# Two expert rounds in one visit, and GpSimd for every key feature

## The chip, the cores and the metric

The kernel runs on one core of a Trainium2 chip. The metric is the device time of one launch in microseconds (us). Three timed runs of the kernel before took 267.41, 268.63 and 268.75 us; the median is 268.63.

## The reference

2048 tokens of width 1024 go through two branches, mixed by a gate per token:

```
g = sigmoid(sum(x * gate_w))                       # one gate per token
a = linear attention(x) @ wo                       # 32 heads of 32
b = x + (one token's expert output, added to its row)
out = g * a + (1 - g) * b
```

In the attention the features of keys and queries are `phi(k) = [softmax(k w_phi), softmax(-k w_phi)]`, 64 numbers a head; `kv = sum over tokens of phi(k) v`, `z = sum of phi(k)`, and each query's output is `phi(q) kv / (phi(q) z)`.

The expert works on one token only: the one with the largest router score `x @ w_r`. Its row `xs` gives `y = (silu(xs @ w_gate) * (xs @ w_up)) @ w_down`, with 3584 hidden columns, times the sigmoid of its score. The three weights are 7.3 MB each, so this branch is mostly a matter of streaming weights.

## The kernel before, in words

**Stages.** First the values of all 16 token tiles (128 tokens each) are computed on TensorE (`k_v`), together with the router and gate scores; in the same stretch `w_phi` is folded into the key and query weights (`fold`, `qfold`), so that later one product gives the features' exponents. `route` and `route_row` find the row index of the expert's token. Then come 32 key steps, `i` = 0 to 31, and 32 query steps with the output product.

**A key step.** One unit `u` is half the heads of one token tile. `feats(u)` issues eight matmuls of 512 columns (L615) into one of two PSUM buffers; ScalarE writes two exponentials (L620, L621) into `e` (four buffers); VectorE sums them (`ssum`, L625) and takes the reciprocal (L629); one engine multiplies (`phi`, L633; six buffers). Which engine does that is chosen at L632: VectorE for unit 3, GpSimd for all others. Five steps later (`LAG`) `k_kv(u)` adds the unit's `phi` times `v` into PSUM with eight small matmuls (L646), for which `phi` is the loaded weight.

**The row index.** `route_row` is called in step 0, after `feats(0)`. VectorE reduces 16 candidates to one number (L367 to L374) and copies it to an integer tile `ixi` (L376). SP loads a register from that tile (L377) and issues the DMA of the token's row (L378). At the very end of the program GpSimd loads the same index into a register for a rarely taken path (L893). `one_hot` and its followers (L386 to L421) turn the index into masks in steps 16 to 23.

**The expert's first two products.** They are done in four rounds, `ffn_gu(r, bufs)`. A round loads weights into buffers, named by letters: W and V are the halves of one buffer, X and Y of another that is free after the value stage, D is one of two buffers that held weights to be folded, A one of a ring of three, of which two hold folded query weights until these are transposed (L331, `qfold_turn`, at steps 4 and 7). Rounds 0 to 2 have four buffers of 1 MB and 32 matmuls of 32 weight columns (L511), round 3 has two buffers and 16 matmuls. Round 1 has a `gate` and an `up` piece in each buffer. Then ScalarE copies the result out (L516), and SP stores it into `gT` (L520), in four DMAs for round 0 and one for each of the others. `GU` says at which steps rounds are visited: 9, 16 and 23, with rounds 2 and 3 together at 23. Round 0's weights are asked for at step 0.

**Order.** The program's order gives priorities. A planner sets the order of each engine's instructions from estimated durations, and puts an instruction that is ready earlier in the program first; on the chip each engine, and SP's queue of DMA issues, runs its list in that order. `tc.issue_after(ins)` adds edges for the planner: what is issued in the block on the engine of `ins` comes behind `ins`.

Of the kernel before, what the change touches and what calls it, by code (L numbers as in the profile page):

```python
# [11 lines left out]
U32 = mybir.dt.uint32  # L12
ALU = mybir.AluOpType
ACTF = mybir.ActivationFunctionType
AX = mybir.AxisListType
PSUM = bass.MemoryType.PSUM
ET = mybir.EngineType

P = 128
S = 2048  # L20
D = 1024
H = 32
DH = 32
# [4 lines left out]
HH = 16  # L28
# [132 lines left out]
def q_heads(wqf, kb, hf):  # L161
    return wqf[:, kb, hf * 512:(hf + 1) * 512].rearrange("p (r c f) -> p c r f", r=4, f=DH)


def _bc(ap, shape):
    return ap.unsqueeze(len(shape) - 1).to_broadcast(shape)
# [3 lines left out]
def kernel(  # L170
# [4 lines left out]
    nc = tc.nc  # L175
# [7 lines left out]
    const = ctx.enter_context(tc.tile_pool(name="const", bufs=1))  # L183
# [78 lines left out]
    moe = {}  # L262
# [101 lines left out]
    def route_row():  # L364
        mrow = moe["mrow"]
        mxv = const.tile([1, 1], F32, name="mxv")
        nc.vector.tensor_copy(out=mxv[:], in_=moe["rs"][0:1, 0:1])  # L367
        nc.vector.tensor_reduce(out=mxv[:], in_=mrow[:, :, 0], axis=AX.X, op=ALU.max)
        cnd = const.tile([1, NT], F32, name="cnd")
        nc.vector.tensor_scalar(out=cnd[:], in0=mrow[:, :, 0], scalar1=mxv[:, 0:1], scalar2=float(2 * S),  # L370
                                op0=ALU.is_lt, op1=ALU.mult)
        nc.vector.tensor_tensor(out=cnd[:], in0=cnd[:], in1=mrow[:, :, 1], op=ALU.add)
        ixf = const.tile([1, 1], F32, name="ixf")
        nc.vector.tensor_reduce(out=ixf[:], in_=cnd[:], axis=AX.X, op=ALU.min)  # L374
        ixi = const.tile([1, 1], U32, name="ixi")
        nc.vector.tensor_copy(out=ixi[:], in_=ixf[:])  # L376
        idx_sp = nc.values_load(ixi[0:1, 0:1], engines=[ET.SP], min_val=0, max_val=S - 1)  # L377
        nc.sync.dma_start(out=rows[0:KB, :], in_=x2[bass.ds(idx_sp, 1), :].rearrange("o (a b) -> (o a) b", b=P))  # L378
        moe["ix"] = (ixi, ixf)
# [43 lines left out]
    def one_hot_row():  # L423
        ixi, ixf = moe["ix"]
        ixm = const.tile([1, 1], F32, name="ixm")
        nc.vector.tensor_copy(out=ixm[:], in_=moe["rs"][0:1, 0:1])
        nc.vector.tensor_single_scalar(out=ixm[:], in_=ixf[:], scalar=float(TOH * P), op=ALU.is_lt)
        nc.vector.tensor_tensor(out=ixm[:], in0=ixm[:], in1=ixf[:], op=ALU.mult)
        ixu = const.tile([1, 1], U32, name="ixu")
        nc.vector.tensor_copy(out=ixu[:], in_=ixm[:])  # L430
        moe["ixu"] = ixu

    def range_flag():
        rm = const.tile([P, 1], F32, name="rm")
        nc.vector.tensor_reduce(out=rm[:], in_=rmn[:], axis=AX.X, op=ALU.min)
        nc.vector.tensor_copy(out=nbb[:, 0:1], in_=rm[:])
# [40 lines left out]
    def ffn_mid():  # L477
        sg = const.tile([P, NFB], F32, name="sg")
        nc.scalar.activation(out=sg[:], in_=ffn_ps[:, 0:28], func=ACTF.Exp, scale=-1.0)
        nc.vector.tensor_scalar_add(out=sg[:], in0=sg[:], scalar1=1.0)  # L480
        nc.vector.reciprocal(out=sg[:], in_=sg[:])
        nc.vector.tensor_tensor(out=sg[:], in0=sg[:], in1=ffn_ps[:, 0:28], op=ALU.mult)
        nc.vector.tensor_tensor(out=hh[:], in0=sg[:], in1=ffn_ps[:, 28:56], op=ALU.mult)

    def gu_load(r, kp, where):
        def part(w, a0, src, k0, nk, col, n):
            nc.sync.dma_start(out=w[:, a0:a0 + nk * n * 512].rearrange("p (k f) -> p k f", k=nk) if n == 4 or nk == 4 else
                              w.rearrange("p (k f) -> p k f", k=2)[:, :, a0:a0 + n * 512],
                              in_=src[:, k0:k0 + nk, col * 512:(col + n) * 512])
        w = wbuf(where)  # L490
        gate_load(w[0:1, 0:1])
        k0 = 2 * kp
        if r == 0:
            part(w, 0, wg_v, k0, 2, 0, 4)
        elif r == 1:
            part(w, 0, wg_v, k0, 2, 4, 3)
            part(w, 1536, wu_v, k0, 2, 0, 1)
        elif r == 2:
            part(w, 0, wu_v, k0, 2, 1, 4)
        else:  # L500
            part(w, 0, wu_v, 4 * kp, 4, 5, 2)
        return w

    def ffn_gu(r, bufs):
        ws = moe.pop("gu0", None) or [gu_load(r, k, b) for k, b in enumerate(bufs)]
        acc = psB.tile([P, 512], F32, name="facc", tag="pB")
        for k, w in enumerate(ws):
            for q in range(2):
                for g in range(4):
                    kb = 4 * k + 2 * q + g // 2 if r == 3 else 2 * k + q  # L510
                    nc.tensor.matmul(acc[32 * g:32 * g + 32, :], lhsT=xs32[:, kb, :],  # L511
                                     rhs=w[:, (q * 4 + g) * 512:(q * 4 + g + 1) * 512], start=(k == 0 and q == 0),
                                     stop=(k == len(ws) - 1 and q == 1),
                                     tile_position=(0, 32 * g), skip_group_check=True)
        gs = wk.tile([P, 512], F32, name="gs", tag="junk", bufs=2)
        nc.scalar.copy(out=gs[:], in_=acc[:])  # L516
        g0 = 16 * r
        step = 4 if r >= 1 else 1
        for g in range(0, 4, step):
            nc.sync.dma_start(out=gT[g0 + 4 * g:g0 + 4 * (g + step), :], in_=gs[32 * g:32 * (g + step):32, :])  # L520
# [89 lines left out]
    def feats(u, wf, is_q):  # L610
        t, hf = divmod(u, 2)
        pk = psA.tile([P, HH, DH], F32, name="pq" if is_q else "pk", tag="pA")
        pkf = pk[:].rearrange("p h f -> p (h f)")
        for kb in range(KB):
            nc.tensor.matmul(pk[:].rearrange("p (c r) f -> p c r f", r=4) if is_q else pkf,  # L615
                             lhsT=xT[:, kb, t * P:(t + 1) * P],
                             rhs=q_heads(wf, kb, hf) if is_q else wf[:, kb, hf * 512:(hf + 1) * 512],
                             start=(kb == 0), stop=(kb == KB - 1))
        e = wk.tile([P, HH, 2, DH], BF, name="e", tag="e", bufs=4)
        nc.scalar.activation(out=e[:, :, 0, :], in_=pk[:], func=ACTF.Exp)  # L620
        nc.scalar.activation(out=e[:, :, 1, :], in_=pk[:], func=ACTF.Exp, scale=-1.0)  # L621
        moe["e"] = e
        e2 = e[:].rearrange("p h s f -> p (h s) f")
        ssum = sm.tile([P, HH * 2], F32, name="ssum", tag="ssum")
        nc.vector.tensor_reduce(out=ssum[:], in_=e2, axis=AX.X, op=ALU.add)  # L625
        if u % 8 == 0:
            moe["rq"] = sm.tile([P, 8, HH * 2], F32, name="rq", tag="rq", bufs=2)
        rs = moe["rq"][:, u % 8, :]
        nc.vector.reciprocal(out=rs, in_=ssum[:])  # L629
        moe["rs"] = rs  # L630
        phi = wk.tile([P, HH, 2, DH], BF, name="phi", tag="phi", bufs=6)
        eng = nc.vector if not is_q and u == 3 else nc.gpsimd  # L632
        eng.tensor_tensor(out=phi[:].rearrange("p h s f -> p (h s) f"), in0=e2,  # L633
                          in1=_bc(rs, [P, HH * 2, DH]), op=ALU.mult)
        if u % 8 == 7:
            g = u // 8 + 4 * is_q
            nc.vector.tensor_reduce(out=rmn[:, g:g + 1], in_=moe["rq"][:].rearrange("p n h -> p (n h)"),
                                    axis=AX.X, op=ALU.min)
        return phi
# [133 lines left out]
                qfold(*PACKS[t, n])  # L773
    LAG = 5
    QT0, QT1 = (4, 7)
    GU = (9, 16, 23)
    TU = 29
    DN, DN2 = NU + 6,3
    TF, TNUM, TWO, TKV = 1.73, 0.27, 1.73, 0.27
# [5 lines left out]
    i = 0  # L785
    while i < 2 * NU or n_next < NU or wos:
        if i in GU:
            r = GU.index(i)
            ffn_gu(r, ('WVAD', 'DXYA', 'WVAD')[r])
            if r == 2:  # L790
                ffn_gu(3, "AA")
        if i == DN - 3:
            nc.scalar.copy(out=hh32[0:1, 0, 0:1], in_=moe["e"][0:1, 0, 1, 0:1])
            nc.scalar.copy(out=hh32[:], in_=hh[:].unsqueeze(2).to_broadcast([P, NFB, 32]))
# [15 lines left out]
        if i < NU:  # L810
            kst[i] = feats(i, wkf, False)
# [7 lines left out]
        if NU <= i < 2 * NU:  # L819
            q_turn(i - NU, feats(i - NU, wqf, True))  # L820
            pe += TF
            fend[i - NU] = pe
# [5 lines left out]
        if i in (QT0, QT1):  # L828
            h = 4 * (i == QT1)
# [3 lines left out]
        if i == TU:  # L833
            ffn_turn()
            ffn_mid()
        if i == 0:
            route_row()
        if i == 7:
            xs_turn()
# [6 lines left out]
        if i == NU + 18:  # L846
            one_hot_row()
# [25 lines left out]
        if pe >= wo_at:  # L873
# [13 lines left out]
            if (t, nh) == (TOH - 1, 1):  # L887
                q_store(0)
                add_row(moe["y2c"][:, 0, :], nc.values_load(moe["ixu"][0:1, 0:1], engines=[ET.Pool], min_val=0,
                                                            max_val=TOH * P - 1))  # L890
        i += 1
    main.close()
    ip = nc.values_load(moe["ix"][0][0:1, 0:1], engines=[ET.Pool], min_val=0, max_val=S - 1)  # L893
    with tc.If(moe["fv"] > 0):
        general_path(tc, A_wqkv, A_w_phi, A_wo, x2, out2, gate, omg, moe["y2c"][:, 1, :], ip, xT, wqf, ident, BDm)
    keep.close()
# [30 lines left out]
```

## Time and profile before

| | |
|---|---|
| timed runs | 267.41, 268.63, 268.75 us |
| profiled execution | 267.2 us, its span 265.5 us |
| TensorE busy | 258.7 us, 97% of the span |
| VectorE busy | 181.4 us, 68% |
| ScalarE busy | 125.9 us, 47% |
| GpSimd busy | 126.3 us, 48% |
| chain that ended last | TensorE 94%, ScalarE 2%, DMA 1%, VectorE 1%, issue 1% |
| DMA | 58.45 MB, mean 220 GB/s |

The span runs from the first to the last instruction of one execution; the execution's own time is 1.7 us longer. Engines are PE (TensorE), PEld (its weight loads), DVE (VectorE), ACT (ScalarE), POOL (GpSimd) and SP (the queue that issues most DMAs). "Chain that ended last" follows the work back from the last instruction, at each step to what released it. The clock granted to TensorE was full in all of the span.

### The profile page before, as it was taken

The page shows a single profiled execution, that of the slowest core. Times are in us where ns is not written, and L with a number is a line of the kernel's source. Part 1 is how long each engine was busy: PE and PEld are TensorE (multiplying, and loading weights), DVE is VectorE, ACT ScalarE, POOL GpSimd, SP SyncE. Part 2 cuts the span into 40 slices and gives each one's busy share as a digit, 9 for nine tenths or more (in the row PEclk, how much of TensorE's full clock was granted, in tenths as well). Part 3 has the DMA queues.
Part 4 walks back from the last instruction along what each step waited for, and adds up shares of the span by engine and source line. Part 5 has one row for each costly group of instructions (what it writes and reads, how often), then busy time and mean ns, then how long its engine had stood idle before and what let it go on. Part 6 is the DMA issues. An engine that isn't in the chain of part 4 may idle for free.

```text
span 265.5 us, 5323 instructions
## 1 busy us (share of the span) xinstructions
PE 258.7 (97%) x1992; PEld 139.3 (52%) x2015; DVE 181.4 (68%) x314; ACT 125.9 (47%) x259; POOL 126.3 (48%) x86
## 2 busy tenths in 40 slices
PE   8999999999999999999999999999999999999994
PEld 3666766765444454545555455455444544544442
DVE  3000323325789785998788789799898797898872
ACT  3153333337864555554556776447362553435210
POOL 6000000000074999579989887655535555455001
PEclk9999999999999999999999999999999999999999
DMA  6989999939999869999969998997999797889642
GB/s 235 247 133 191 165 190 187 173 78 329 395 348 199 204 101 399 398 336 333 358 232 338 147 247 180 219 202 137 254 216 202 150 236 145 202 150 201 158 120 67
DMA packets 110970, 58.45 MB, mean 220 GB/s; under 512 B 93580, under 2 KB 98780, under 8 KB 110940
## 3 DMA queue, kind: packets, MB, share of 16 engines
q1 hardware_dynamic: 108140, 53.39, 82.9%
q10 hardware_dynamic: 2768, 4.67, 6.6%
q8 instruction: 17, 0.28, 0.4%
q14 instruction: 13, 0.11, 0.1%
q0 software_dynamic: 32, 0.00, 0.0%
HBM read 31.27 MB, written 4.20 MB: 134 GB/s over the span
## 4 chain that ended last, share of the span: by engine, by line
PE 94%; ACT 2%; DMA 1%; DVE 1%; issue 1%; DVEq 0%
PE pq L615 21%; PE po L719 21%; PE pk L615 19%; PE pv L575 18%; PE kvps L646 3%; PE num L680 3%; PE facc L511 2%; PE pW L311 1%; PE pv L597 1%; PE small_ps L529 1%; DMA shv<-in_A_x_dram 1%; PE kvps L597 1%; ACT kvps L335 1%; DVE wfT L328 0%; PE kvps L323 0%
## 5 line engine op out<-in xcount | busy, mean ns | idle before, releaser
L633 POOL TENSOR_TENSOR phi<-e,rq 128x1024 bf16<-128x1024 bf16 x63 | 119.6, 1913 | 66.0 <-DVE rq L629 48.4
L625 DVE TENSOR_REDUCE ssum<-e 128x32 f32<-128x1024 bf16 x64 | 77.4, 1210 | 14.6 <-ACT e L621 14.5
L615 PEld LDWEIGHTS <-xT 128*128 128x128 bf16 x512 | 47.3, 97 | 52.6 <-issue 1.4
L615 PE MATMUL pq<-wqf,xT 128*128 128x512 bf16 x256 | 60.3, 379 | 0.0
L615 PE MATMUL pk<-wkf,xT 128*128 128x512 bf16 x245 | 59.4, 379 | 0.6
L719 PE MATMUL po<-wo_sb,oT 128*128 128x512 bf16 (+2 forms) x252 | 58.4, 372 | 0.6
L575 PE MATMUL pv<-wv_sb,xT 128*128 128x256 bf16 (+2 forms) x336 | 51.1, 307 | 0.0
L575 PEld LDWEIGHTS <-xT 128*128 128x128 bf16 x336 | 31.7, 97 | 15.3 <-issue 0.5
L582 ACT CAST v_all<-pv 128x384 bf16<-128x384 f32 (+1 forms) x45 | 20.1, 448 | 35.2 <-PE pv L575 29.4
L719 PEld LDWEIGHTS <-oT 128*128 128x128 bf16 x264 | 23.9, 98 | 23.3
L620 ACT ACTIVATE e<-pq 128x512 bf16<-128x512 f32 x32 | 18.9, 592 | 36.2 <-PE pq L615 35.7
L313 DVE CAST wkf<-pW 128x512 bf16<-128x512 f32 x16 | 10.3, 686 | 32.9 <-PE pW L311 32.9
L620 ACT ACTIVATE e<-pk 128x512 bf16<-128x512 f32 x32 | 19.1, 597 | 28.5 <-PE pk L615 21.9
L723 DVE SCALAR_TENSOR_TENSOR oo<-po,gate,xg 128x512 bf16<-128x512 f32 (+2 forms) x33 | 24.0, 728 | 4.4 <-PE po L719 4.3
L453 POOL COPY wch<-shv 1x1 bf16<-1x1 bf16 x3 | 0.4, 178 | 53.8 <-DMA shv<-in_A_wqkv_dram 53.8
L629 DVE RECIPROCAL rq<-ssum 128x32 f32<-128x32 f32 x64 | 21.8, 342 | 1.3
L685 DVE TENSOR_TENSOR o_sb<-num,rden 128x512 bf16<-128x512 f32 x32 | 21.6, 674 | 0.8
L621 ACT ACTIVATE e<-pk 128x512 bf16<-128x512 f32 x32 | 18.9, 592 | 0.0
L621 ACT ACTIVATE e<-pq 128x512 bf16<-128x512 f32 x32 | 18.9, 590 | 0.0
L704 ACT ACTIVATE xg<-xin,omg 128x1024 f32<-128x1024 bf16 x16 | 18.4, 1149 | 0.4
L680 PEld LDWEIGHTS <-phT 128*128 128x128 bf16 x256 | 12.4, 98 | 7.8 <-issue 0.5
L646 PEld LDWEIGHTS <-phi 128*128 128x128 bf16 x256 | 11.8, 98 | 7.6 <-issue 0.8
(132 smaller groups left out, 151.9 us busy)
## 6 DMA issues: line engine op xcount, KB each, us to landing
wch<-in_B_w_down_dram SPq DMA_DIRECT2D x7, 1024.0 KB
wch<-in_B_w_up_dram SPq DMA_DIRECT2D x6, 1024.0 KB
wch<-in_B_w_gate_dram SPq DMA_DIRECT2D x4, 1024.0 KB
xin<-in_A_x_dram ACTq DMA_DIRECT2D x16, 256.0 KB
out_dram<-oo SPq DMA_DIRECT2D x30, 128.0 KB
wch<-in_B_w_gate_dram SPq DMA_DIRECT2D x4, 768.0 KB
wv_sb<-in_A_wqkv_dram SPq DMA_DIRECT2D x8, 256.0 KB
wo_sb<-in_A_wo_dram SPq DMA_DIRECT2D x1, 2048.0 KB
```

The source lines that it names most:

```text
L575: nc.tensor.matmul(pv[:, 0:hi - lo], lhsT=xT[:, kb, t * P:(t + 1) * P], rhs=wv_sb[:, kb, lo:hi], start=(kb == 0), stop=(kb == KB - 1))
L582: nc.scalar.copy(out=v_all[:, t, h0:h1, 0:DH], in_=pv[:, 0:(h1 - h0) * DH].rearrange("p (h d) -> p h d", d=DH))
L615: nc.tensor.matmul(pk[:].rearrange("p (c r) f -> p c r f", r=4) if is_q else pkf, lhsT=xT[:, kb, t * P:(t + 1) * P], rhs=q_heads(wf, kb, h ...
L620: nc.scalar.activation(out=e[:, :, 0, :], in_=pk[:], func=ACTF.Exp)
L621: nc.scalar.activation(out=e[:, :, 1, :], in_=pk[:], func=ACTF.Exp, scale=-1.0)
L625: nc.vector.tensor_reduce(out=ssum[:], in_=e2, axis=AX.X, op=ALU.add)
L629: nc.vector.reciprocal(out=rs, in_=ssum[:])
L633: eng.tensor_tensor(out=phi[:].rearrange("p h s f -> p (h s) f"), in0=e2, in1=_bc(rs, [P, HH * 2, DH]), op=ALU.mult)
L680: nc.tensor.matmul(num[:, pl * 66:pl * 66 + 66], lhsT=phT[:, pl, :], rhs=KV[hf][:, pl, :], start=True, stop=True)
L685: nc.vector.tensor_tensor(out=st["o"][:, hf * HH:(hf + 1) * HH, :].rearrange("p (r h) d -> p r h d", h=2), in0=nv[:, :, :, 0:DH], in1=rden ...
L719: nc.tensor.matmul(po[:, 0:w], lhsT=st["oT"][:, kb, :], rhs=moe["wo"][:, kb, sl], start=(kb == 0), stop=(kb == KB - 1))
L723: nc.vector.scalar_tensor_tensor(out=o_out[:, 0:w], in0=po[:, 0:w], scalar=gate[:, t:t + 1], in1=st["xg"][:, sl], op0=ALU.mult, op1=ALU.add)
```

## The change

Rounds 0 and 1 of the expert are visited together at step 14 (rounds 2 and 3 stay at 23). GpSimd multiplies unit 3 too. `route_row` is called in step 1 instead of step 0. Each key unit's sum is issued behind the reciprocal of the unit before, and unit 2's behind the copy of the index to `ixi`. A second integer copy of the index, `ixl`, is made in query step 18, behind that unit's reciprocal, and GpSimd's register load at the end of the program reads it instead of `ixi`.

```diff
@@ route_row
-        nc.vector.tensor_copy(out=ixi[:], in_=ixf[:])
+        moe["rec"] = nc.vector.tensor_copy(out=ixi[:], in_=ixf[:]).ins
@@ one_hot_row
         moe["ixu"] = ixu
+        ixl = const.tile([1, 1], U32, name="ixl")
+        with tc.issue_after(moe["rec"]):
+            nc.vector.tensor_copy(out=ixl[:], in_=ixf[:])
+        moe["ixl"] = ixl
@@ feats
-        nc.vector.tensor_reduce(out=ssum[:], in_=e2, axis=AX.X, op=ALU.add)
+        with tc.issue_after(moe["rec"]) if "rec" in moe and not is_q else ExitStack():
+            nc.vector.tensor_reduce(out=ssum[:], in_=e2, axis=AX.X, op=ALU.add)
...
-        nc.vector.reciprocal(out=rs, in_=ssum[:])
+        moe["rec"] = nc.vector.reciprocal(out=rs, in_=ssum[:]).ins
...
-        eng = nc.vector if not is_q and u == 3 else nc.gpsimd
-        eng.tensor_tensor(out=phi[:].rearrange("p h s f -> p (h s) f"), in0=e2,
-                          in1=_bc(rs, [P, HH * 2, DH]), op=ALU.mult)
+        nc.gpsimd.tensor_tensor(out=phi[:].rearrange("p h s f -> p (h s) f"), in0=e2,
+                                in1=_bc(rs, [P, HH * 2, DH]), op=ALU.mult)
@@ main loop
-    GU = (9, 16, 23)
+    GU = (14, 23)
...
-            r = GU.index(i)
-            ffn_gu(r, ('WVAD', 'DXYA', 'WVAD')[r])
-            if r == 2:
-                ffn_gu(3, "AA")
+            r = 2 * GU.index(i)
+            ffn_gu(r, ("WVAD", "WVAD")[r // 2])
+            ffn_gu(r + 1, ("DXYA", "AA")[r // 2])
...
-        if i == 0:
+        if i == 1:
             route_row()
...
-    ip = nc.values_load(moe["ix"][0][0:1, 0:1], engines=[ET.Pool], min_val=0, max_val=S - 1)
+    ip = nc.values_load(moe["ixl"][0:1, 0:1], engines=[ET.Pool], min_val=0, max_val=S - 1)
```

## Rows read from the trace of the kernel before

**Rows 1.** Windows: engines' busy us, granted clock, DMA share, GB/s.
```profile
68.20:252.97 184.77, 183.45 (x1407) 91.57 (x1416) 157.05 (x266) 97.48 (x183) 120.34 (x66) 1.00 0.93 237
```

**Rows 2.** Chain that ended last: start us, us, what (xcount); start and key stage.
```profile
0.88 3.25 DMA shv<-in_A_x_dram
...
81.19 0.26 PE kvps L646 x8
...
83.18 0.27 PE kvps L646 x8
...
89.11 0.25 PE kvps L646 x8
...
101.00 1.84 PE facc L511 x32
...
114.85 0.25 PE kvps L646 x8
...
121.63 0.28 PE kvps L646 x8
```

**Rows 3.** Groups by line, 77 to 138 us: busy, mean ns, idle before.
```profile
L633 DVE TENSOR_TENSOR phi<-e,rq 128x1024 bf16<-128x1024 bf16 x1 | 2.0, 1979 | 0.0
```

**Rows 4.** GpSimd in order of time: start us, us, what [idle before, releaser].
```profile
73.02 1.91 POOL L633 TENSOR_TENSOR phi<-e,rq 128x1024 bf16<-128x1024 bf16 x1 [13.54 <-DVE rq L629]
76.81 3.78 POOL L633 TENSOR_TENSOR phi<-e,rq 128x1024 bf16<-128x1024 bf16 x2 [1.88 <-DVE ixi L376]
...
84.33 5.65 POOL L633 TENSOR_TENSOR phi<-e,rq 128x1024 bf16<-128x1024 bf16 x3 [3.74 <-ACT e L621]
```

**Rows 5.** VectorE in order of time, the index chain among units 1 and 2.
```profile
74.11 0.84 DVE L370 TENSOR_SCALAR cnd<-mrow,mxv 1x16 f32<-1x16 f32 x1
74.99 0.16 DVE L372 TENSOR_TENSOR cnd<-cnd,mrow 1x16 f32<-1x16 f32 x1
...
76.31 0.35 DVE L629 RECIPROCAL rq<-ssum 128x32 f32<-128x32 f32 x1
76.58 0.08 DVE L376 CAST ixi<-ixf 1x1 uint32<-1x1 f32 x1
76.59 1.21 DVE L625 TENSOR_REDUCE ssum<-e 128x32 f32<-128x1024 bf16 x1
...
77.84 0.35 DVE L629 RECIPROCAL rq<-ssum 128x32 f32<-128x32 f32 x1
```

**Rows 6.** ScalarE, end of unit 1's exponentials.
```profile
72.96 0.61 ACT L621 ACTIVATE e<-pk 128x512 bf16<-128x512 f32 x1
```

**Rows 7.** VectorE and GpSimd in order of time, 107 to 114 us.
```profile
107.98 1.91 POOL L633 TENSOR_TENSOR phi<-e,rq 128x1024 bf16<-128x1024 bf16 x1 [1.16 <-DVE hl L390]
...
108.20 1.72 DVE L394 CAST hlb<-hl 1x2 bf16<-1x2 uint32 x1
...
111.59 3.78 POOL L633 TENSOR_TENSOR phi<-e,rq 128x1024 bf16<-128x1024 bf16 x2 [1.69 <-DVE er L397]
...
112.91 0.60 DVE L405 TENSOR_TENSOR hlc<-hlc,iot 128x1 f32<-128x1 f32 x1
```

**Rows 8.** SP's DMA issues in order of time, 78 to 101 us.
```profile
78.16 0.38 SPq L378 DMA_DIRECT2D rows<-in_A_x_dram  x1
...
79.11 5.72 SPq L331 DMA_TRANSPOSE wqf<-wfT  x4
...
87.31 7.62 SPq L331 DMA_TRANSPOSE wqf<-wfT  x4
94.98 2.60 SPq L520 DMA_DIRECT2D gT<-gs  x4
97.62 3.23 SPq L487 DMA_DIRECT2D wch<-in_B_w_up_dram  x6
```

**Rows 9.** Windows again, while rounds 1 to 3 are loaded (columns as in rows 1).
```profile
98.00:100.00 2.00, 2.00 (x18) 1.05 (x17) 1.57 (x2) 1.10 (x3) 2.00 (x2) 1.00 0.63 158
104.00:116.80 12.80, 12.70 (x104) 6.46 (x107) 10.69 (x20) 6.72 (x13) 8.51 (x5) 1.00 1.04 398
```

## The prediction, made before the changed kernel was built

> **What bounds the kernel now.** I read the stage windows first, then the chain of waits, then the engines' rows around the places that the change touches. From 68.20 us, where the key steps begin, to 252.97, where only the last output matmuls are left, TensorE is busy for 183.45 of 184.77 us [rows 1]: 1.32 us is idle in 185. The chain of waits stays on TensorE there too. One key step (eight 512-column feature matmuls and eight small KV matmuls) takes 1.99 us from one KV group to the next (81.19 to 83.18) [rows 2]. VectorE, ScalarE, GpSimd and the transfers are all beside that. So an edit of the key stage can win at most the idle 1.32 us and whatever TensorE work it removes, and lose whatever it makes TensorE wait.
>
> **One expert visit fewer.** The expert work moves, it doesn't shrink: 112 matmuls before and after. A visit has a fixed part. The visit at step 9 (32 matmuls) lies between the KV groups at 83.18 and 89.11, 5.93 us, where two plain steps take 3.98: it costs 1.95. The one at step 23 (48 matmuls) lies between 114.85 and 121.63, 6.78 us: it costs 2.80 [rows 2]. So 16 matmuls cost 0.85, one 0.053, and the fixed part is 1.95 - 32 x 0.053 = 0.25 us. Two visits become one: -0.25.
>
> **The multiply of unit 3 goes to GpSimd.** VectorE loses one multiply of 1.98 us [rows 3] and GpSimd gets one more, of 1.91 us [rows 4]. VectorE's time is not on the chain: worth 0 by itself. GpSimd stood idle for 3.74 us just there, waiting for unit 4's inputs [rows 4], because VectorE was busy with unit 3; that gap now takes the multiply. From then on GpSimd gives one unit in 1.91 us against TensorE's 1.99, so it doesn't fall behind. What hides it is the distance of five steps between a unit's features and its KV matmuls; at the first units this cover is thin, and the next part is about that.
>
> **The row index, one step later.** The index chain (L367 to L376) moves from behind step 0 to behind step 1, and two ordering edges are added: unit 1's sum goes behind unit 0's reciprocal, unit 2's sum behind the index copy. What is queued behind that copy on VectorE is therefore every later key sum, and GpSimd's multiplies wait for those. Before, the chain and the sums were mixed: L370 and L372, then unit 1's sum, L374, unit 1's reciprocal, the copy at 76.58, unit 2's sum at 76.59 and its reciprocal at 77.84 [rows 5]. After: unit 1's exponentials end at 73.57 [rows 6], its sum of 1.2 us runs to 74.8, its reciprocal of 0.35 to 75.2, and GpSimd multiplies unit 1 from 75.25 to 77.16. GpSimd's register load, which held unit 1 until 76.81 [rows 4], is out of the way. But L370 now comes at about 75.6, inside that multiply. In the rows L370 took 0.84 us for 16 numbers and ended at 74.95, when GpSimd's multiply of unit 0 (73.02 + 1.91 = 74.93) had just ended [rows 4, 5]. The 1x2 cast L394 took 1.72 and ended at 109.92, with GpSimd's multiply ending at 109.89; L405 ended at 113.51, and GpSimd's first of two multiplies at about 113.5 [rows 7]. So I let L370 wait until 77.16, then L372, L374 and the copy go to about 77.65, unit 2's sum to 78.86, its reciprocal to 79.25, its multiply from 79.35 to 81.26. The KV matmuls of unit 2 began at 81.19 [rows 2]. After 81.26 come a handover, for which the rows show 0.15 (unit 1's reciprocal ended at 76.66, its multiply began at 76.81 [rows 4, 5]), and the weight load, which I put at twice that: TensorE starts at about 81.7, +0.5. Unit 3 follows at 83.17 against a KV group now due at 83.7, unit 4 at 85.1 against 85.7: no second wait. Low end: L370 isn't held, the copy is done by 76.3, and the wait is 0 (unit 2's multiply ends by 79.9). High end: L372, which like L405 has two SBUF inputs, is caught as well and takes L405's 0.60, so 1.1. I take 0.5, since four small instructions in the rows ended with a multiply.
> The Trainium skill (SBUF — State Buffer, "Who interferes with whom") says that VectorE and GpSimd share one pair of SBUF ports, locked for a whole instruction; a tensor_scalar in a two-port mode or a two-input tensor_tensor takes it, a tensor_reduce never does. The rows agree (L370, L394 and L405 end with a multiply, the sums keep their 1.2 us). By that rule the sum has the +0.5; were the long L370 an accident, it would have 0.
>
> **The register load behind the key features.** It costs the added 1x1 copy on VectorE (the like copy L376 took 0.08 [rows 5]) in the query stage, where the chain is on TensorE: 0. What it frees is at most those 0.15 us of unit 1, which no KV group waited for: 0.
>
> **The transfers.** SP issues in order. Its index DMA (78.16) came behind the copy at 76.66; if the copy comes at 77.65, SP's next work moves by 1.0: both groups of four transposes, the second of which ran from 87.31 to 94.93 [rows 8]. Round 0's weights were all issued by then, and it now has five more steps: 0. Round 1's last piece (256 KB) was issued at 97.62, behind four small stores of round 0's result (2.60 us) [rows 8]. In 98 to 100 us the queue moved 2 x 158 = 316 KB [rows 9], so the piece had landed by about 99.8, 2.2 after its issue. These stores now come later, so that the piece can follow the transposes at 95.95 and land at 98.2. When is it needed? The eighth KV group comes at 83.18 + 5 x 1.99 + 0.5 = 93.6, then eight feature matmuls (1.99 less the group's own 0.25, so 1.74) and the group itself to 95.6, round 0 (32 x 0.053 = 1.7) to 97.3, three quarters of round 1 to 98.6. Spare: 0.4, so 0. High end: if the first transposes take as long as the second (7.62 instead of 5.72 [rows 8]), 1.9 is lost and the wait is 1.5. Rounds 2 and 3 need 6.3 MB, issued from about 97.3 as round 0's buffers come free, against 97.6 to 104.6 before; at 398 GB/s [rows 9] that is 15.8 us from about 98.5, done at 114.3, with the visit at 116.8: 0.
>
> **The sum.** The profiled execution took 267.2 us (span 265.5 and 1.7 around it). -0.25 + 0.5 = +0.25, so 267.45 for an execution like it. It is shorter than the timed ones (267.41, 268.63, 268.75; median 268.63). Between 68 and 253 us there is no wait of such a size that another execution could have more of, while the chain begins with a transfer of 3.25 us [rows 2] that the change doesn't touch; so I take this spread to stay and set the base at the mean of the four, 268.0, which is 0.8 above the profiled one. Forecast 268.2. Its own bounds: 267.2 - 0.25 = 266.95, and 267.2 - 0.25 + 1.1 + 1.5 + 0.8 = 270.35.
>
> **Rivals.**
> A. *No cost at all.* L370 is not held, or the planner places it where GpSimd is idle; only the visit's 0.25 shows: 266.95 + 0.8 = 267.75. For it: GpSimd is idle often at the first units [rows 4]. Against: three held instructions [rows 5, 7].
> B. *The long executions are cured.* If the 268.6 to 268.7 executions hold a late expert load or a GpSimd wait that the profiled one escaped, earlier loads remove it, and all come out like the shortest: 267.2 - 0.25 = 267.0. For it: round 1's last piece had only some 2.5 us to spare before (landed 99.8, needed at 101.0 + 1.3 = 102.3 [rows 2]). Against: nothing in the profile waits there.
> C. *Slower: the stores stay in front.* If the planner, which puts what is earlier in the program first, keeps round 0's four stores ahead of round 1's last piece on SP, they wait for round 0's result (97.3 and a copy of 0.6), take 2.60, and the piece is issued at 100.5 and lands at 102.7, where it is needed at 98.6: +4.1, and 268.2 + 4.1 = 272.3. It decides as soon as the piece lands after 98.6. For it: that order stood before [rows 8]. Against: then round 0's result was long there when SP came free; now SP is free at about 96, before it.
> D. *GpSimd becomes the pace.* Its margin is 0.08 us a step. If holds by VectorE eat it over the first 14 steps, with no visit at step 9 to catch up, 14 x 0.08 = 1.1 is lost: 269.3.
>
> **Chances.** Forecast 0.40, A 0.21, B 0.19, C 0.12, D 0.08. About 0.5% (1.34 us, so 267.29 and 269.97) is what a measurement of this kernel can tell from no change. Faster is B and a little of A: 0.21. Slower is C and the upper tail of the forecast: 0.15. Same: 0.64. The range 266.9 to 270.3 holds all but C and little else; the likeliest case's own is 266.95 to 270.35.
>
> **What would show it.** In the new trace: the L511 group at about 95.5 with 64 matmuls and nothing at 85; two plain steps around it longer by 3.7 instead of 1.95 twice; L370 near 1.5 us long, ending with unit 1's multiply; the KV group of unit 2 about 0.5 late; the piece of round 1 issued right behind the transposes. I am wrong if TensorE has a gap of over 1 us before 138 us, or if the start before 15 us differs, which I hold untouched.

## The result and the profile after

The changed kernel takes 269.73 us (median of 9 runs), the kernel before 268.63 (9 runs beside it). One run of each was a slow one (962.61 and 303.8 us); the ratio of the fast runs is 1.0053 [1.0035, 1.0071] (the two medians alone give 1.0041), so the changed kernel is slower by 0.9 to 1.9 us. Timed again later: 269.5 against 268.09, ratio 1.0052 [1.003, 1.0075]. The forecast was 268.2.

| | before | after |
|---|---|---|
| profiled execution, span | 267.2, 265.5 us | 269.26, 267.6 us |
| first KV group to last output matmul | 77.07 to 261.67: 184.60 | 77.11 to 262.61: 185.50 |
| last output matmul to the end of the span | 3.9 | 5.0 |
| TensorE busy | 258.7 | 260.2 |
| VectorE, GpSimd busy | 181.4, 126.3 | 180.7, 128.3 |

The stage window of the changed kernel, from the start of the key steps to the last output matmuls (columns as in [rows 1]):

```profile
68.20:253.89 185.69, 185.02 (x1431) 91.72 (x1416) 156.36 (x266) 97.63 (x183) 122.29 (x67) 1.00 0.93 235
```

The clock is full and TensorE is idle for 0.67 us only, against 1.32 in [rows 1], yet time is lost. The trace of before lacks 23 matmul records (1992 beside 2015 weight loads; the one of after has 2015 of each), so a part of its 1.32 was never idle time. Idle sums don't settle this case; distances between like instructions do. TensorE in order of time (start us, us, operation, idle before and what ended it), first two KV groups of the kernel before, then the changed kernel. Its lines moved down by four, so L650 is the KV group of [rows 2]; a group starts some 0.15 us earlier here than in the chain view of [rows 2], which counts it from the end of the work before it.

```profile
79.05 0.42 PE L646 MATMUL kvps<-v_all,phi 128*128 128x66 bf16 x8
...
81.03 0.42 PE L646 MATMUL kvps<-v_all,phi 128*128 128x66 bf16 x8
```
```profile
79.09 0.42 PE L650 MATMUL kvps<-v_all,phi 128*128 128x66 bf16 x8
...
81.52 0.43 PE L650 MATMUL kvps<-v_all,phi 128*128 128x66 bf16 x8 [0.28 <-POOL phi L637]
...
93.45 0.42 PE L650 MATMUL kvps<-v_all,phi 128*128 128x66 bf16 x8
...
95.52 3.42 PE L515 MATMUL facc<-wch,xs 128*32 128x512 bf16 x59
99.22 0.59 PE L515 MATMUL facc<-wch,xs 128*32 128x512 bf16 x5 [0.29 <-DMA wch<-in_B_w_up_dram]
99.75 0.43 PE L650 MATMUL kvps<-v_all,phi 128*128 128x66 bf16 x8
```

There are two new waits. Unit 2's KV group comes 2.43 us after unit 1's, where a plain step takes 1.98 (79.05 to 81.03 before): 0.45 lost to GpSimd. The six groups after it, to 93.45, follow every 1.99 us, so GpSimd doesn't fall behind. And the merged visit stops for the last weights of round 1. From the KV group at 93.45 to that at 99.75 are 6.30 us; two plain steps would be 3.96 and the merged visit, where nothing waits, costs 3.66 beyond one of them (shown below by five kernels), so 1.98 + 3.66 = 5.64 was due and 0.66 is lost. The bracket names only 0.29 of it: five matmuls waited, and the record of the matmul before them, 0.38 us long, covers the rest.

The chain that ended last, near the visit, shows what was waited for (SPq is SP's queue of issues):

```profile
96.17 3.02 DMA wch<-in_B_w_up_dram
...
99.22 0.59 PE facc L515 x5
```

The piece was issued right behind the last transpose, as foreseen, but took 3.02 us to land. SP's list answers to [rows 8]:

```profile
79.37 0.38 SPq L378 DMA_DIRECT2D rows<-in_A_x_dram  x1
...
80.42 5.46 SPq L331 DMA_TRANSPOSE wqf<-wfT  x4
87.84 0.39 SPq L491 DMA_DIRECT2D wch<-in_B_w_gate_dram  x1
88.35 7.77 SPq L331 DMA_TRANSPOSE wqf<-wfT  x4
96.17 2.94 SPq L491 DMA_DIRECT2D wch<-in_B_w_up_dram  x3
99.21 3.21 SPq L524 DMA_DIRECT2D gT<-gs  x5
```

The index DMA comes 1.2 us later than before (79.37 against 78.16) and the transposes end 1.2 later (96.12 against 94.93). The stores of `gT` stand behind the piece, not ahead of it. VectorE and GpSimd, answering to [rows 5] and [rows 4]:

```profile
75.65 1.68 DVE L370 TENSOR_SCALAR cnd<-mrow,mxv 1x16 f32<-1x16 f32 x1
77.36 0.17 DVE L372 TENSOR_TENSOR cnd<-cnd,mrow 1x16 f32<-1x16 f32 x1
...
77.76 0.14 DVE L376 CAST ixi<-ixf 1x1 uint32<-1x1 f32 x1
77.83 1.20 DVE L630 TENSOR_REDUCE ssum<-e 128x32 f32<-128x1024 bf16 x1
79.06 0.35 DVE L634 RECIPROCAL rq<-ssum 128x32 f32<-128x32 f32 x1
```
```profile
75.39 1.91 POOL L637 TENSOR_TENSOR phi<-e,rq 128x1024 bf16<-128x1024 bf16 x1 [0.43 <-DVE rq L634]
79.56 22.48 POOL L637 TENSOR_TENSOR phi<-e,rq 128x1024 bf16<-128x1024 bf16 x12 [2.25 <-DVE rq L634]
```

L370 ends at 77.33, GpSimd's multiply of unit 1 at 77.30: 16 numbers were held for 1.68 us. Unit 2's sum stands behind the copy, and GpSimd gets its factors only at 79.41.

Where do the 3.02 us of the piece go? Windows of the changed kernel around it, then of the kernel before (columns as in [rows 1]; the last is GB/s):

```profile
95.80:97.40 1.60, 1.60 (x36) 0.80 (x32) 1.19 (x3) 0.97 (x2) 1.60 (x2) 1.00 1.17 240
97.40:98.80 1.40, 1.40 (x31) 0.54 (x20) 0.98 (x2) 0.59 (x1) 1.40 (x2) 1.00 0.62 190
98.80:99.20 0.40, 0.14 (x3) 0.00 (x0) 0.00 (x0) 0.00 (x0) 0.40 (x1) 1.00 0.00 0
```
```profile
94.60:96.20 1.60, 1.55 (x15) 0.84 (x14) 1.28 (x2) 1.05 (x2) 1.60 (x2) 1.00 1.18 241
...
98.60:100.00 1.40, 1.40 (x15) 0.77 (x14) 1.22 (x2) 0.89 (x2) 1.40 (x2) 1.00 0.90 224
```

In both kernels a block of 1.6 us at 240 GB/s begins 0.3 us before SP has issued the last transpose: most of that data moves *after* its issue ends. In the changed kernel the piece follows at once: 1.2 us until the transpose's bytes are through, 1.4 at 190 GB/s for 256 KB (1.4 x 190 = 266 KB), and 0.4 between the last byte and TensorE's release. It seems as if the transposes made its landing slow, but the packets say otherwise. The piece is 256 packets of 1 KB. These lines count packets that start in a stretch: in the kernel before from 98.70 to 99.80 and from 98.70 to 100.33, then in the changed kernel from 97.38 to 98.82.

```profile
DMA packets 238, 0.25 MB, mean 227 GB/s; under 512 B 6, under 2 KB 234, under 8 KB 238
DMA packets 301, 0.38 MB, mean 234 GB/s; under 512 B 16, under 2 KB 272, under 8 KB 301
```
```profile
DMA packets 320, 0.27 MB, mean 187 GB/s; under 512 B 64, under 2 KB 320, under 8 KB 320
```

"Under 2 KB" less "under 512 B" is the piece: 228, 256 and 256 packets. By the trace's packet records its first packet starts 1.09 us after its issue in the kernel before, where the queue was nearly empty (4 to 6 GB/s from 96.20 to 98.60), and 1.23 after it in the changed kernel, behind the transposes. Its last packet ends 2.70 after the issue before (at 100.32) and 2.64 after it in the changed kernel (at 98.81). So the piece takes as long in a nearly empty queue as behind the transposes.

### The profile page after: what moved, and what is told of

Its sections match the earlier page's. It is cut to its first block, busy times and chain, and to the rows that moved or that the text cites. A ratio compares the mean times of both kernels' runs of the same rounds, so it can differ in the third digit from the quotient of the medians.

```text
span 267.6 us, 5347 instructions
## 1 busy us (share of the span) xinstructions
PE 260.2 (97%) x2015; PEld 139.5 (52%) x2015; DVE 180.7 (68%) x314; ACT 126.1 (47%) x259; POOL 128.3 (48%) x87
## 4 chain that ended last, share of the span: by engine, by line
PE 87%; DVE 4%; ACT 2%; DMA 2%; SPq 1%; POOL 1%; issue 0%; DVEq 0%; ACTq 0%; POOLq 0%
PE pq L619 21%; PE po L723 21%; PE pv L579 18%; PE pk L619 15%; PE num L684 3%; PE kvps L650 3%; SPq L331 1%; DVE ssum L630 1%; PE pW L311 1%; PE pv L601 1%; PE facc L515 1%; DMA shv<-in_A_x_dram 1%; PE small_ps L533 1%; PE kvps L601 1%; DMA wch<-in_B_w_up_dram 1%; POOL phi L637 1%
## 5 line engine op out<-in xcount | busy, mean ns | idle before, releaser
L637 POOL TENSOR_TENSOR phi<-e,rq 128x1024 bf16<-128x1024 bf16 x64 | 121.6, 1912 | 65.0 <-DVE rq L634 53.4
L630 DVE TENSOR_REDUCE ssum<-e 128x32 f32<-128x1024 bf16 x64 | 77.4, 1209 | 17.0 <-ACT e L625 16.9
L723 PE MATMUL po<-wo_sb,oT 128*128 128x512 bf16 (+2 forms) x264 | 60.0, 372 | 0.0
L650 PEld LDWEIGHTS <-phi 128*128 128x128 bf16 x256 | 11.8, 98 | 7.9 <-POOL phi L637 1.2
```

Of the source, the lines that this page charges most:

```text
L637: nc.gpsimd.tensor_tensor(out=phi[:].rearrange("p h s f -> p (h s) f"), in0=e2, in1=_bc(rs, [P, HH * 2, DH]), op=ALU.mult)
L723: nc.tensor.matmul(po[:, 0:w], lhsT=st["oT"][:, kb, :], rhs=moe["wo"][:, kb, sl], start=(kb == 0), stop=(kb == KB - 1))
```

## The experiments

The base is the same for all: a kernel whose two new waits are removed should stand 0.2 us below the kernel before. Each run's time is compared with the kernel before on the same chip; "stretch" is the time from the first KV group to the last output matmul in its profile (184.60 and 184.63 in the two profiles of before). The first theory says that unit 2's wait and the piece's wait are all; the rivals put the loss elsewhere: the merged visit as such, GpSimd's pace, or the end of the program.

**Three visits again.** The changed kernel with its visits back at the old steps.

```diff
-    GU = (14, 23)
+    GU = (9, 16, 23)        # and the loop's three lines as before
```

> The changed kernel with its visits put back to steps 9, 16 and 23. Theory T (two waits): the changed kernel loses 0.5 us where unit 2's KV matmuls wait for GpSimd, because L370 is held by unit 1's multiply, and 0.75 us in the visit at step 14, where the last weight piece of round 1 lands at 99.2 us; the merged visit itself saves 0.25. Here the wait in the visit goes and the saving goes with it: the last matmul, at 262.6 us in the changed kernel, ends at 262.1; the time is 0.5 below the changed kernel and 0.45 above the kernel before. Rival P (pace): GpSimd, multiplying every unit without the visit at step 9 to catch up, slows the key steps as a whole; then the visit at 9 gives it all back, and the last matmul ends at 261.9 or earlier. Rival E (end): 1.1 us of the profiled difference lies after the last matmul (5.0 us there against 3.9) and belongs to the change; then the time stays within 0.3 of the changed kernel although the last matmul ends earlier, and the stretch after it stays near 5.0.

268.41 against 268.14: 1.0009 [0.9993, 1.0024], stretch 185.06. Unit 2's group still waits (79.37 to 81.80, 0.45), and no visit does. So the other edits together cost 0.46 in the stretch, and the rest of the loss hangs on the merged visit. GpSimd does all 64 multiplies here too, and behind unit 2 no group waits for it.

**The merged visit alone,** in the kernel before.

```diff
-    GU = (9, 16, 23)
+    GU = (14, 23)           # and the changed loop's lines
```

> The kernel before with rounds 0 and 1 together at step 14 and nothing else. T: the piece of round 1 goes out at about 95.0 and lands 3.0 later, at 98.0, before it is needed. But VectorE still multiplies unit 3, so that GpSimd ends unit 4 at 86.2 as before, where its KV matmuls are now due at 85.2 (the visit at step 9 covered that): a wait of 1.2, less the visit's 0.25. Last matmul at 261.67 + 0.95 = 262.6, time 0.9 above the kernel before. If the merged visit is costly by itself, a wait of over 0.5 shows inside the visit too; if the visit at step 9 covered nothing, the last matmul ends at 261.4 and the time is 0.25 below the kernel before.

269.4: 1.0036 [1.002, 1.0051], stretch 185.67. TensorE in order of time:

```profile
83.14 0.41 PE L646 MATMUL kvps<-v_all,phi 128*128 128x66 bf16 x8
...
86.39 0.43 PE L646 MATMUL kvps<-v_all,phi 128*128 128x66 bf16 x8 [1.11 <-POOL phi L633]
...
94.33 0.42 PE L646 MATMUL kvps<-v_all,phi 128*128 128x66 bf16 x8
...
99.97 0.43 PE L646 MATMUL kvps<-v_all,phi 128*128 128x66 bf16 x8
```

Here the visit waits for nothing: 99.97 - 94.33 - 1.98 = 3.66, against 1.95 for one single visit in [rows 2] and 1.93 from KV group to KV group (83.04 to 86.95 in the kernel before), so one visit fewer saves 0.2. But unit 4's group is 1.27 late, for GpSimd. The three multiplies from 84.33 in [rows 4], behind VectorE's unit 3, were covered by the visit at step 9, which TensorE now reaches five steps later. The changed kernel has no such wait. It differs at this place by the multiply's move to GpSimd and by the sums that stand behind reciprocals; one of the two, or both, make up for the merged visit's missing cover at unit 4. They were not tried apart.

**The visit one step later,** at 15.

```diff
-    GU = (14, 23)
+    GU = (15, 23)
```

> The changed kernel with the merged visit one step later, at 15. T: the piece of round 1 still lands at about 99.2 and is needed at about 100.6, so its wait of 0.75 goes: last matmul at 261.85, time 0.75 below the changed kernel, 0.2 above the kernel before. The wait of 0.5 at unit 2 stays. Rival P: the merged visit is just as long, last matmul at 262.6. A third way: rounds 2 and 3, loaded 2 us later, come late at step 23, and the wait moves there (last matmul 262.6 or later, with a gap at about 118).

268.6: 1.002 [1.0004, 1.0036], stretch 184.83.

```profile
95.81 0.42 PE L650 MATMUL kvps<-v_all,phi 128*128 128x66 bf16 x8
...
101.46 0.43 PE L650 MATMUL kvps<-v_all,phi 128*128 128x66 bf16 x8
```

101.46 - 95.81 - 1.98 = 3.67: with 2 us more, the piece is there in time. What is left is unit 2's 0.45 less 0.2.

**No edge behind the index copy.** Unit 2's sum need not wait for the copy.

```diff
-        moe["rec"] = nc.vector.tensor_copy(out=ixi[:], in_=ixf[:]).ins
+        nc.vector.tensor_copy(out=ixi[:], in_=ixf[:])
```

> The changed kernel without the edge that puts unit 2's sum behind the index copy. VectorE's list then has unit 2's sum between L368 and L370, and its reciprocal between L370 and L372. T: unit 2's multiply starts at about 77.9 instead of 79.56, and its KV matmuls don't wait: the 0.5 goes, while the wait in the visit at step 14 stays at 0.75 if SP's transposes end as late as now. Last matmul at 262.1, time 0.5 below the changed kernel. If L372, which has two SBUF inputs, is caught by unit 2's multiply instead, unit 3's sum is late in turn and its KV matmuls wait about as long: last matmul at 262.6. Rival P: nothing changes, 262.6, with the KV matmuls late all along.

269.49: 1.0068 [1.0045, 1.0091], stretch 185.98. Neither expectation had this. Unit 2's wait is gone (its group comes at 81.05), and the visit takes 3.66, but the small matmul L383, which needs the token's row, stands on TensorE ahead of unit 3's group:

```profile
84.62 0.18 PE L383 MATMUL small_ps<-ident,rows 128*128 128x8 bf16 x1 [1.43 <-DMA rows<-in_A_x_dram]
84.66 0.41 PE L650 MATMUL kvps<-v_all,phi 128*128 128x66 bf16 x8
```

Without the edge the chain slips between later units: L370 is held by unit 2's multiply, the copy comes 2.9 us later than in the changed kernel, and the planner puts two transposes ahead of the row's DMA. VectorE and SP:

```profile
77.81 1.36 DVE L370 TENSOR_SCALAR cnd<-mrow,mxv 1x16 f32<-1x16 f32 x1
...
80.69 0.13 DVE L376 CAST ixi<-ixf 1x1 uint32<-1x1 f32 x1
```
```profile
78.53 3.05 SPq L331 DMA_TRANSPOSE wqf<-wfT  x2
83.24 0.39 SPq L378 DMA_DIRECT2D rows<-in_A_x_dram  x1
```

The edge has a purpose, then: it spares unit 3 a wait of 1.6 us (84.66 - 81.05 - 1.98) for 0.45 at unit 2, given that the chain starts in step 1.

**The index chain back in step 0,** edges kept.

```diff
-        if i == 1:
+        if i == 0:
             route_row()
```

> The changed kernel with the row index computed in step 0 again, still followed by an edge (which now puts unit 1's sum behind the index copy). T: L370 starts at about 74.1, inside unit 0's multiply, and is held for 0.84 as in the kernel before; the copy comes at 75.5, unit 1's multiply runs from 77.2 to 79.1, and its KV matmuls, due at 79.05, wait about 0.35; unit 2 doesn't wait. SP is 2 us earlier, the piece of round 1 goes out at about 94.3 and lands at 97.3, before it is needed: no wait in the visit. Last matmul at 261.7 to 261.8 (changed kernel: 262.6), time 0.8 below the changed kernel, within 0.3 of the kernel before. Rival: if the late piece doesn't hang on the index chain, the visit keeps its 0.75 and the last matmul ends at 262.4.

269.19: 1.0044 [1.0028, 1.0061], stretch 185.85. L370 is caught by unit 0's multiply (73.68, 1.28, to 74.96), which holds nobody that TensorE needs soon: unit 1's group is 0.09 late, unit 2's not at all. But the visit still waits, longer than in the changed kernel's first profile:

```profile
96.33 3.15 DMA wch<-in_B_w_up_dram
```

The piece is as late as in the changed kernel although SP had the index early, and TensorE, with no wait at unit 2, arrives sooner. The wait is 5.01 - 3.66 = 1.35. So the late piece does not hang on the index chain alone, which was the rival's case. TensorE's 0.45 at unit 2 had covered a part of it.

**GpSimd's register load as before,** reading `ixi`.

```diff
-    ip = nc.values_load(moe["ixl"][0:1, 0:1], ...)
+    ip = nc.values_load(moe["ix"][0][0:1, 0:1], ...)
```

> The changed kernel with GpSimd's register load reading the first copy of the index again; the load then stands behind GpSimd's multiplies of units 0 and 1 and waits for the index copy at 77.8. T: unit 2's multiply can't start before 79.5 anyway, so nothing changes: 185.5 from the first KV group to the last matmul, time as the changed kernel's. Rival: the load holds GpSimd longer than the sums do, unit 2's KV matmuls come later than 0.5 behind, and the stretch is 185.8 or more.

269.58: 1.0045 [1.0026, 1.0065], as the changed kernel. Unit 2's wait is 0.44 again, the visit's 1.2. The load's place is worth nothing that can be measured.

**The visit one step earlier,** at 13.

```diff
-    GU = (14, 23)
+    GU = (13, 23)
```

> The changed kernel with the merged visit one step earlier, at 13: nothing is moved on SP, so the piece of round 1 still goes out at 96.2 and lands at 99.2. T: the visit starts one step (1.98) earlier and its wait grows by as much, from 0.75 to about 2.7; last matmul at 262.6 + 2.0 = 264.6. Rival: the extra time of the visit at 14 is a cost of the visit itself (more matmuls in a row, two accumulations): then it stays what it is, and the last matmul stays at 262.6.

271.56: 1.013 [1.01, 1.016] (2 runs), stretch 189.08. The piece is issued at 96.30 and lands 2.96 later, as at 14, while TensorE is there 2 us sooner:

```profile
93.68 3.42 PE L515 MATMUL facc<-wch,xs 128*32 128x512 bf16 x59
99.30 0.59 PE L515 MATMUL facc<-wch,xs 128*32 128x512 bf16 x5 [2.21 <-DMA wch<-in_B_w_up_dram]
```

The visit takes 6.24, so the wait is 6.24 - 3.66 = 2.58. Another 1.7 us beyond it is a matter of the clock (last section).

**Before and after once more,** the first for one profiled execution and the second timed.

> The kernel before, profiled once more, to see the stretch after the last matmul. In its first profile this was 3.9 us, in the changed kernel and the four experiments 4.6 to 5.0. T: that stretch varies from one execution to the next and isn't the change's; a second profile shows 4.6 to 5.0 with the last matmul again at 261.7 +- 0.3. Rival E: it is 3.9 again, and the change adds 1.1 us behind the last matmul.

> The changed kernel again, beside the others on one chip. T: first KV group to last matmul 185.5 +- 0.2, with the waits of 0.5 at unit 2 and about 0.75 in the visit; time 0.9 to 1.4 above the kernel before (0.35 to 0.5%). Rival E: the two waits don't repeat and the time is lost behind the last matmul.

The kernel before took 267.57 us in this execution, and its profile had 3.87 us after the last output matmul, as the first: it did not show the longer end that was expected. The changed kernel, timed again: 269.5, 1.0052 [1.003, 1.0075], stretch 186.29; the piece was issued at 97.33 and took 3.21, and the visit waited 5.09 - 3.66 = 1.43. The wait differs from one execution to the next because the end of the transposes does (96.1 and 97.3 here; 94.9 and 95.8 in the two profiles of before, where nobody waits for it). Of the 1.2 us between the two, 0.6 are the whole execution's (its first KV group comes at 77.70, not 77.11); the other 0.6 and the 0.2 that the piece took longer are the difference of the waits.

**Step 0 and no edge,** the index chain in step 0 and no edge behind its copy, in the changed kernel.

> The changed kernel with the row index in step 0 and without the edge behind its copy: merged visit, GpSimd for unit 3 and the edges between sums and reciprocals stay. VectorE's list up to unit 2 is then that of the kernel before. T: no KV group waits (unit 2's multiply ends at about 80.6, unit 4's at 84.4, due at 85.1); the piece of round 1 goes out at about 95.0 and lands at 98.0 to 98.2, needed at 98.1: a wait of 0 to 0.2. Last matmul at 261.4 to 261.6, 0.1 to 0.25 earlier than in the kernel before; a time that can't be told from it. Rival P: GpSimd falls behind without the visit at step 9 even so, and the last matmul ends at 262 or later.

268.24 against 268.16: 1.0001 [0.9984, 1.0018], stretch 185.03. No wait at unit 2 and none for the row; the piece is issued at 95.56 and lands 3.00 later, and the visit waits 0.54.

**The second transposes one step later,** in the changed kernel.

```diff
-    QT0, QT1 = (4, 7)
+    QT0, QT1 = (4, 8)
```

> The changed kernel with one number changed: the second group of four transposes is asked for at step 8 instead of 7. SP's list then has the last piece of round 1 (256 KB) ahead of these transposes instead of behind them, and the order of TensorE's instructions is the same. Counted from the first KV group to the end of the last matmul, the kernel before takes 184.6 us and the changed kernel 185.5. T: the piece goes out at about 88.3 and has landed by 92, so the visit at step 14 doesn't wait; its 0.75 goes, the 0.5 at unit 2 stays: 184.8, time 0.75 below the changed kernel. Rival: the wait in the visit is for something else that came last by chance: 185.5.

268.63 against 268.09: 1.0019 [1.0002, 1.0036], stretch 184.84. SP's list and TensorE:

```profile
89.15 0.46 SPq L491 DMA_DIRECT2D wch<-in_B_w_up_dram  x1
89.72 7.85 SPq L331 DMA_TRANSPOSE wqf<-wfT  x4
```
```profile
94.20 0.42 PE L650 MATMUL kvps<-v_all,phi 128*128 128x66 bf16 x8
...
99.85 0.43 PE L650 MATMUL kvps<-v_all,phi 128*128 128x66 bf16 x8
```

The piece now goes ahead of the transposes: its last packet ends at 93.74, and TensorE needs it 3.04 us into the visit (98.56 less 95.52 in the changed kernel), at 99.32. So 3.67 for the visit, no wait. This is the direct test of the cause: same visit, same step, same order on TensorE; what differs is SP's list, the piece ahead of the transposes and not behind them.

**All three together:** index chain in step 0, no edge, transposes one step later.

> Merged visit, GpSimd for unit 3, the edges between sums and reciprocals, the row index in step 0 without the edge behind it, and the second group of transposes at step 8: both waits of the changed kernel taken away, the saving of the merged visit kept. T: first KV group to last matmul 184.4 (kernel before 184.6), the visit 3.66 beyond a plain step; a time 0.2 below the kernel before, too little to be told from it. If GpSimd falls behind after all, or rounds 2 and 3 come late, 185 or more.

267.91 against 268.09: 0.9996 [0.9979, 1.0012], stretch 184.41, the shortest of all. None of the waits is left, and what remains of the change is its 0.2, too little to be told from no change.

The waits, as the profiles show them, against the stretches and the times (us). "Sum" is all waits, less 0.2 for a merged visit; "stretch" what the profile's stretch has over 184.6; "timed" is ratio less 1, times 268.1, with its interval:

| kernel | unit 2 | visit | other | sum | stretch | timed |
|---|---|---|---|---|---|---|
| changed | 0.45 | 0.66 | | 0.9 | 0.9 | 1.4 [0.9, 1.9] |
| changed, again | 0.45 | 1.43 | | 1.7 | 1.7 | 1.4 [0.8, 2.0] |
| three visits | 0.45 | not merged | | 0.45 | 0.5 | 0.2 [-0.2, 0.6] |
| merged visit alone | 0 | 0 | 1.27, unit 4 | 1.1 | 1.1 | 1.0 [0.5, 1.4] |
| visit at 15 | 0.45 | 0 | | 0.2 | 0.2 | 0.5 [0.1, 1.0] |
| no copy edge | 0 | 0 | 1.63, unit 3 | 1.4 | 1.4 | 1.8 [1.2, 2.4] |
| index in step 0 | 0 | 1.35 | 0.09, unit 1 | 1.2 | 1.2 | 1.2 [0.8, 1.6] |
| old register load | 0.44 | 1.2 | | 1.4 | 1.4 | 1.2 [0.7, 1.7] |
| visit at 13 | 0.44 | 2.58 | 1.66, clock | 4.5 | 4.5 | 3.5 [2.7, 4.3] |
| step 0, no edge | 0 | 0.54 | | 0.3 | 0.4 | 0.0 [-0.4, 0.5] |
| transposes later | 0.44 | 0 | | 0.2 | 0.2 | 0.5 [0.1, 1.0] |
| all three | 0 | 0 | | -0.2 | -0.2 | -0.1 [-0.6, 0.3] |

The named waits make up every stretch to 0.1 us: whatever else changed in it comes to no more than that. One profile is one execution, and the piece's wait varies between executions, as do the parts before and behind the stretch, so the times need not match as closely; all but "visit at 13" lie within about 0.5 of the sum.

## Why the prediction was wrong

Most of its steps came out as it put them; one term of the sum was mis-sized. The time, 269.73, lies in its range (266.9 to 270.3), whose upper end allowed for this wait, but the sum was +0.25 where 0.9 to 1.9 were timed.

**One expert visit fewer, -0.25.** Five kernels without a wait show 3.66 or 3.67 for the merged visit, two single ones cost 1.93 each: -0.2. Right.

**The row index, one step later, +0.5.** L370 at 75.65, held to the end of unit 1's multiply, the copy at 77.76, unit 2's group 0.45 late: the mechanism is right. That the size is so close is in part luck: unit 2's multiply ended at 81.47 instead of 81.26, and TensorE started 0.05 behind it, where 0.45 had been allowed. The index in step 0 takes that wait away. The Trainium skill (SBUF — State Buffer, "Who interferes with whom") has VectorE and GpSimd share a port pair, locked for a whole instruction; in the two runs that moved L370, it ended again with a multiply, at 74.96 against 74.93 (step 0) and 79.17 against 79.14 (no edge). The two-input L372, which the high bound would have had caught, was not: by then GpSimd was idle.

**The multiply of unit 3 goes to GpSimd, and the register load: 0.** Right as sizes: no wait comes from GpSimd's pace, so rival D is out, and the old load costs nothing. But the rows were read wrongly in one place: [rows 4] name the index copy as what GpSimd waited for ahead of unit 1, and I took that for the register load. The kernel with step 0 and no edge loads its register from `ixl` at the end, and yet GpSimd starts unit 1 at the same 76.81, with the same name in the bracket:

```profile
76.81 3.78 POOL L637 TENSOR_TENSOR phi<-e,rq 128x1024 bf16<-128x1024 bf16 x2 [1.88 <-DVE ixi L376]
```

So the load never held that unit. Unit 1's reciprocal ends at 76.66, as the copy does, and GpSimd waited for that. What the merged visit alone does to unit 4, the prediction did not price.

**The transfers: "Spare: 0.4, so 0".** This is the term that failed. The mechanism was named (the piece behind the transposes, the point 98.6 at which it is needed, the bound of a wait up to 1.5); mis-sized was the time from the piece's issue to its landing, put at 2.2 and measured at 3.02. The 2.2 was a wrong reading of [rows 9]: the 316 KB that the queue moved from 98 to 100 us are in part bytes of the loads behind the piece. By 99.80, when it "had landed", 28 of its 256 packets had not started, and the last ended 2.70 after the issue. Then come the 0.4 until TensorE is released. With these 3.1 the trace of before gives a landing at 95.95 + 3.1 = 99.05 for a need at 98.6: a wait of 0.45, not a spare of 0.4. The issue came at 96.17 instead of 95.95, which adds the other 0.2. TensorE reached the point at 99.22 - 0.66 = 98.56, just as worked out. So the cost was 0.66, and 1.43 in an execution whose transposes end 0.6 us later against TensorE and whose piece takes 0.2 longer. With it the sum is -0.2 + 0.45 + 0.66 to 1.43 = 0.9 to 1.7 on top of the kernel before, as timed. Moving the piece ahead of the transposes takes this term away.

**The base.** The forecast set the profiled 267.2 up by 0.8 to 268.0, the mean of four; the timed median beside the changed kernel was 268.63, and 268.14 and 268.09 (34 runs each) and 268.16 (21) in later ones. That was a fair base and not the error.

**Rivals.** A and B fell with the two waits. C did not come: SP's list has the piece, two loads and then the stores. Its rule ("it decides as soon as the piece lands after 98.6") held, though, by another cause than the stores. B's "2.5 us to spare before" rests on the same 99.8; 100.32 and the 0.4 until the release make it 1.6.

**What stays open.** The end, from the last output matmul, is 3.9 us in both profiles of before and 4.0 to 5.2 in those of the changed kernels; the start, up to the first KV group, varies from 77.1 to 77.9. Both profiles of before are of short executions (267.2 and 267.57, where the timed medians are 268.1 to 268.6). If the longer end were a cost of the change, "step 0, no edge" (5.2 there, 0.4 in the stretch) would be 1.7 us slower than before and "three visits" (4.85 there) 1.4; they were timed at 0.0 [-0.4, 0.5] and 0.2 [-0.2, 0.6]. So the loss is not there, but what makes the end differ is not settled. Nor is what sets the end of the second transposes (94.2 to 97.3 between executions). How the piece's 3.02 us divide was read from windows and packets and not tested by itself, and unit 3 back on VectorE in the changed kernel was not tried.

## What to carry to other kernels

A load's landing time is taken from its own packets, to the last one, and the consumer's release comes after that (0.4 us here). The bytes that a queue moved in a window belong in part to the loads behind it. When work that waited for several things is merged to one place, list its last input with issue, landing and need, and treat a spare smaller than the spread of that issue between executions as a wait. An edge that looks like a cost may buy an earlier start elsewhere, so remove it only together with what made it necessary.

## What the runs showed of the hardware

TensorE's granted clock fell after a single wait. In the kernel with the visit at 13, where TensorE idled 2.21 us before 99.30 (windows, columns as in [rows 1]):

```profile
98.00:100.00 2.00, 0.70 (x11) 0.28 (x11) 0.00 (x0) 0.07 (x1) 2.00 (x2) 1.00 0.72 155
100.00:102.00 2.00, 1.95 (x13) 0.82 (x12) 0.00 (x0) 0.52 (x1) 0.29 (x1) 0.65 0.92 346
102.00:104.00 2.00, 2.00 (x13) 1.00 (x12) 0.00 (x0) 0.69 (x2) 0.00 (x0) 0.50 1.02 418
104.00:106.00 2.00, 2.00 (x18) 1.04 (x17) 1.54 (x2) 0.68 (x2) 0.00 (x0) 1.00 1.03 381
```

0.50 is the 1.2 GHz level. The next two steps took 3.18 and 2.44 us instead of 1.98, so the wait of 2.58 cost 1.66 more. In the changed kernel, whose waits were 0.66 and 1.43, the clock stayed at 1.00.

A hold by GpSimd's multiply does not follow the size of VectorE's instruction: inside one multiply of the changed kernel (the second of these two, 108.93 to 110.84) a 1x1 instruction ran in 0.14 us and a 1x2 cast, a moment later, took 1.72, to the multiply's end. The sum of 128x1024 numbers (L630) is not held: it took 1.20 us at 77.83, with GpSimd idle, and 1.16 at 80.79, beside its multiplies.

```profile
106.88 3.96 POOL L637 TENSOR_TENSOR phi<-e,rq 128x1024 bf16<-128x1024 bf16 x2
```
```profile
108.97 0.14 DVE L392 TENSOR_SCALAR hl<-ixi 1x1 uint32<-1x1 uint32 x1
109.14 1.72 DVE L394 CAST hlb<-hl 1x2 bf16<-1x2 uint32 x1
```
